# A channel attention kernel (384 x 384 x 384): the order of the second pass planned anew, and other row pitches in DRAM

## The chip, the cores and the metric

The kernel runs on one core of a Trainium2 chip. The metric is the device time of one execution in microseconds (us); lower is better. The kernel before takes 719.73 us, the median of three runs (719.13 to 720.23).

## The reference

```python
def reference(x, w1d):                       # x: (1, 384, 384, 384) bf16, w1d: (1,) bf16
    g = jnp.einsum("bhwc->bc", x) / (H * W)  # mean of each channel over all pixels
    s = _sigmoid(g * w1d[0])                 # k = 1: one tap
    return x * s[:, None, None, :]
```

(The padding and the loop over the taps are left out, since there is one tap.) The scale of each channel is known only when all of x has been summed. So x is read once for the sums, and every value has to be multiplied and written afterwards. x has 147,456 pixels of 384 channels, 113 MB in bf16, far more than the core's SBUF holds.

## The kernel before

**Rows.** A "row" is here one pixel (384 channels, 768 bytes) in each of the 128 partitions, 98,304 bytes together. A partition has 1,152 rows (`RPP`). The SBUF tile `arena` holds 275 of them (`ROWS`). DRAM is split in two chunks: `STREAMED`, the first 128 x 784 pixels, in which a partition's 784 rows lie behind one another, and `KEPT`, the other 128 x 368 pixels, with 368 rows a partition. So neighbouring partitions lie 784 or 368 rows apart in DRAM.

**First pass.** SP issues all loads on one queue. TensorE sums the rows as they land (`sum_rows`, one matmul with a matrix of ones for each row, accumulated in `bank0`). The streamed rows are loaded, summed and overwritten. The 368 kept rows stay on the core. Of these 72 (`N_RAW`) stay as they are, and 296 are packed in ten groups of 4q rows, q being 8 for eight "pair" groups (1 to 8), 6 for the group `BANKED` (9) and 4 for the group `FIRST` (0): VectorE folds each fourth row of a group into spare exponent bits of the three others (`fold`), in pieces of 4 rows (`PIECE`), so that 3q rows hold 4q. ScalarE tests that the exponents allow it and leaves the results in `seen`. The group `BANKED` is moved to PSUM. The odd groups lie in one column of the arena from row 12 up to `U` (108), the even ones in another from `G0` (116) up to `V` (212); each group's unfolded fourth quarter goes to the q rows just above its three quarters, which are the first rows of the group above it in the column, or the rows `U` to `U`+8 or `V` to `V`+8 at the top. The rows `A` (220), `T` (259) and `Y` (267) and up to 275 follow; `T` and `Y` are scratch.

**The turn.** ScalarE makes the scale `s_bf` from the sums (L445 to 449) and copies it to PSUM as `s_ps`.

**Second pass.** Everything in it is one multiplication by `s_bf` (`scale`, L461, on VectorE; three pieces of 4 rows at the start on GpSimd), then a store. The 72 raw rows come first. `unfold` takes a group's pieces apart again: with p = 4 a piece is five bit operations of 4 rows, one of 12, three joins of 4, and the multiplications of 12 and of 4. The 784 streamed rows are loaded again, scaled and stored, in the arena's free rows. These are few at first (47, as 204 hold folded groups, 16 wait for fourth quarters and 8 are scratch) and more with every group that has left.

**The planner.** The order of the second pass is worked out while the program is built: a loop steps a model clock by `DT` = 0.05 us and decides what VectorE does next and which load or store SP issues next, by model costs: `ROW` for a row moved, `PER_LOAD` and `PER_STORE` for a transfer, `SEEN` until a finished transfer is noticed, `TS` and `TT` for VectorE. What comes out is a fixed order of instructions on each engine, with semaphore waits; on the chip SP issues its transfers in that order, each as soon as what it needs is done. The class `Flow` records the steps and derives the waits.

In the planner before, VectorE scales landed rows while the backlog of transfers is below `PENDING` = 24 us, and otherwise starts a group. A store goes out as soon as its rows are scaled. A load is issued when a run of at least 32 idle rows is there (up to 48), or 8 rows with less than 9 us of backlog, or any with less than 4 us. The groups are taken alternately from the two columns: 7, 8, 5, 6, BANKED, 3, 4, 1, 2, FIRST. The first two are stored in two parts (12 and 20 rows), the others whole.

**The fallback.** `again` (L549) is a branch on GpSimd that redoes the kept rows where a test of `fold` failed. Its first instruction reads the flag. `Flow.emit` attaches one of a step's waits to the instruction that the step returns; `again` returns none (L568), so that one wait is left out.

Of the kernel before, what the change touches and what calls it, by code (L numbers as in the profile page):

```python
# [11 lines left out]
class Step:  # L12
    __slots__ = ("eng", "emit", "dma", "lane", "deps", "wanted", "rank", "waits", "know", "i")

    def __init__(self, eng, emit, dma):
        self.eng, self.emit, self.dma = eng, emit, dma
        self.deps, self.wanted, self.rank, self.waits, self.know = [], False, 0, [], None
        self.lane = None


class Flow:
# [12 lines left out]
    def add(self, eng, emit, reads=(), writes=(), dma=False, after=()):  # L34
        s = Step(eng, emit, dma)
        s.i = len(self.steps)
# [31 lines left out]
    def emit(self):  # L68
# [36 lines left out]
        last = {}  # L105
        with self.tc.tile_critical():  # L106
            for s in self.steps:
# [20 lines left out]
def kernel(  # L128
# [85 lines left out]
    STREAMED, KEPT = (0, N_STREAM), (N_STREAM, N_KEPT)  # L214
# [260 lines left out]
    def unfold(k, first):  # L475
# [10 lines left out]
        def fields():  # L486
            bits(u, w0, SHR, 4, AND, 0x0780, wc[0], uc)
            bits(b, w1, SHR, 8, AND, 0x0078, wc[1], bc)
            join(u, u, b, OR, uc + bc, uc)

        def signs():
            bits(c, w2, SHR, 12, AND, 0x0007, wc[2], cc)
            bits(b, w2, SHL, 4, AND, 0x8000, wc[2], bc)
            join(u, u, c, OR, uc + cc, uc)

        def three():
            wall = wc[0] + wc[1] + wc[2]
            bits(w, w, AND, 0x87FF, OR, 0x3800, wall, wall)
            join(u, u, b, OR, uc + bc, uc)
            scale(a, 3 * p)  # L500

        def fourth():

            bits(u, u, XOR, FIX, AND, 0xFFFF, uc, uc)
            scale(at, p + more)

        return [
            (fields, 2 * TS(p) + TT(p)),
            (signs, 2 * TS(p) + TT(p)),
            (three, TS(3 * p) + TT(p) + TT(3 * p)),  # L510
            (fourth, TS(p) + TT(p + more)),
# [68 lines left out]
    now = dve_at = 0.0  # L580
    moves, waiting, over, acts = deque(), deque(), deque(), deque()
    landed = deque()
    idle = [False] * ROWS
    todo = 0
    last_is_load = False

    def release(a, n):
        for i in range(a, a + n):
            idle[i] = True

    def runs():
        got, i = [], 0
        while i < ROWS:
            if idle[i]:
                j = i
                while j < ROWS and idle[j]:
                    j += 1
                got.append((j - i, i))
                i = j
            else:  # L600
                i += 1
        return got

    def send(chunk, a, lo, hi, then, known=None):

        waiting.append((dve_at, hi - lo, then, chunk, a, lo, [] if known is None else known))

    def backlog():
        return sum(e[1] for e in moves) + ROW * sum(e[1] for e in waiting)

    def split(n, m):
        k = -(-n // m)
        cuts = [n * i // k for i in range(k + 1)]
        return list(zip(cuts, cuts[1:]))


    SCRATCH = rows(Y, 8)
    needed = [set(SCRATCH + rows(U, 8)), set(SCRATCH + rows(V, 8)), set(SCRATCH)]

    def stored(a, n):  # L620

        def f():
            for i in range(a, a + n):
                for left in needed:
                    left.discard(("a", i))
                if not Y <= i < Y + 8 and not U <= i < U + 8 and not V <= i < V + 8:
                    idle[i] = True
        return f


    for a, n in (
        *((Y + i, 2) for i in range(0, 8, 2)), *((T + i, 2) for i in range(0, 8, 2)), (A + 26, 6), (A + 32, 7), (A + 13, 13), (V + 4, 4), (A, 13)
    ):
        landed.append((KEPT, a, raw(a), n, True))


    alongside = deque()
    t = 1.0
    for a, n in ((U, 4), (U + 4, 4), (V, 4)):
        scale(a, n, "POOL", after=[copied])  # L640
        t += 0.2 + 0.84 * n
        alongside.append((t, KEPT, a, raw(a), n))
# [5 lines left out]
    home = {g: i for i, column in enumerate(COLUMNS) for g in column}  # L648
    home[BANKED] = 2
    free = [True, True, True]  # L650
    total = len(GROUPS)
    out_rows = 0
    turns = deque()
    bank_at = None
    since = None
# [3 lines left out]
    def start_group():  # L659

# [3 lines left out]
        column = home[g]  # L664
        if needed[column] or not free[column] or g == BANKED and (bank_at is None or now < bank_at[1]):
            return False
        line.popleft()
        free[column] = False
        a, q = GROUPS[g]
        if g == BANKED:  # L670
            a = bank_at[0]

        below = 0
        if column < 2 and g != COLUMNS[column][0]:
            below = GROUPS[COLUMNS[column][COLUMNS[column].index(g) - 1]][1]

        def part():
            release(a + below, sent - below)

        def done():  # L680
            nonlocal out_rows
            out_rows += 1
            free[column] = True
            release(a + max(below, sent), n_rows - max(below, sent))

        for k in of_group(g):
            turns.extend(step + (None,) for step in unfold(k, a))
        sent, n_rows = 0, 4 * q + (g == BANKED)
        if len(line) >= total - N_SPLIT and q == PAIR:

            f, t, _ = turns[-6]
            sent = 3 * PIECE
            turns[-6] = (f, t, lambda: send(KEPT, a, c_group[g], c_group[g] + sent, part, written))
        f, t, _ = turns[-1]
        turns[-1] = (f, t, lambda: send(KEPT, a + sent, c_group[g] + sent, c_group[g] + n_rows, done, written))
        return True

    while True:

        if dve_at <= now:  # L700
            ahead = backlog()
            can = bool(turns)
            if not can and not alongside and (ahead >= PENDING or not landed):
                can = start_group()
            if landed and (ahead < PENDING or not can):
                chunk, a, lo, n, end = landed.popleft()
                scale(a, n, s=s_ps if alongside and now else s_bf)
                dve_at = now + TT(n)
                since = (a, lo) if since is None else since
                if end or ahead < MERGE:  # L710
                    b, first = since
# [99 lines left out]
```

## Time and profile before

| | us |
|---|---|
| median of the three runs | 719.73 |
| the profiled execution, its own time | 719.59 |
| its span, first to last instruction | 717.8 |
| VectorE busy in the span | 495.0 |
| TensorE busy | 212.8 |
| ScalarE busy | 116.5 |
| GpSimd busy | 9.4 |

The first pass ends at about 268 us with the activation that makes the scale (start 267.76 us). The page's slices are the span in 40 equal parts of 17.9 us. "SPq" is SP's queue of transfer instructions: a row of it gives the start of a stretch of issues, its length and their count. "[3.86 <-DMA ...]" behind a row is the idle time of that engine before it and what ended it. "DMA share" is the mean busy share of the core's 16 transfer engines; it can exceed 1 by some per cent in short windows. The 16 engines work each through its own part (8 partitions) of every transfer, in the order of the issues.

### The profile page before, as it was taken

What the parts mean: (1) busy time and instruction counts of PE and PEld (TensorE: products, weight loads), DVE (VectorE), ACT (ScalarE), POOL (GpSimd) and SP (SyncE); (2) the same over time, 40 slices, a digit from 0 to 9 for tenths busy, and PEclk for the clock granted to TensorE, in tenths of its full rate; (3) what the DMA queues carried; (4) which work ended last, traced back from release to release, by engine and by line L of the source; (5) the groups of instructions that cost most, each with busy time, mean ns of one, the idle gap of its engine ahead of it and who ended that gap; (6) DMA issues with size and microseconds to landing.
All of it is one profiled execution on the core that took longest, in us unless ns stands there. A gap on an engine that the chain in (4) does not pass through costs nothing.

```text
span 717.8 us, 2069 instructions
## 1 busy us (share of the span) xinstructions
PE 212.8 (30%) x1202; PEld 0.3 (0%) x3; DVE 495.0 (69%) x475; ACT 116.5 (16%) x97; POOL 9.4 (1%) x7
## 2 busy tenths in 40 slices
PE   4667879988787880000000000000000000000000
PEld 0000000000000000000000000000000000000000
DVE  4600001988998839989999999899999796035910
ACT  3700001666777620001000000000000000000000
POOL 0000000000000004000000000000000000000000
PEclk9898989999998995555555555555555555555555
DMA  9999999999999989999999999999999999999997
GB/s 378 438 438 436 438 436 419 437 431 426 423 430 425 429 331 389 404 432 423 429 428 433 431 431 430 432 429 443 428 435 430 429 436 434 436 432 432 434 433 314
DMA packets 20029, 303.69 MB, mean 423 GB/s; under 512 B 2226, under 2 KB 3506, under 8 KB 6578
## 3 DMA queue, kind: packets, MB, share of 16 engines
q1 hardware_dynamic: 20016, 303.57, 99.1%
q8 instruction: 4, 0.07, 0.0%
q14 instruction: 7, 0.06, 0.0%
q10 hardware_dynamic: 2, 0.00, 0.0%
HBM read 190.32 MB, written 113.25 MB: 423 GB/s over the span
## 4 chain that ended last, share of the span: by engine, by line
DMA 61%; DVE 22%; PE 8%; ACT 2%; issue 1%; SPq 0%; another core or an unknown queue 0%; DVEq 0%
DMA arena<-in_x_dram 47%; DVE arena L461 16%; DMA out_dram<-arena 14%; PE bank L241 8%; DVE arena L275 4%; ACT arena L312 2%; DVE arena L281 2%; SPq L235 0%; SPq L471 0%; ACT s_bf L448 0%; DVEq L112 0%; SPq L806 0%; SPq L112 0%; SPq L106 0%
## 5 line engine op out<-in xcount | busy, mean ns | idle before, releaser
L461 DVE TENSOR_TENSOR arena<-arena,s_bf 128x1536 bf16<-128x1536 bf16 (+9 forms) x96 | 228.4, 2411 | 70.7 <-DMA arena<-in_x_dram 58.0
L275 DVE TENSOR_SCALAR arena<-arena 128x1536 uint16<-128x1536 uint16 (+2 forms) x247 | 145.4, 634 | 106.8 <-DMA arena<-in_x_dram 100.7
L241 PE MATMUL bank<-arena,ones 128*128 128x384 bf16 x1151 | 204.5, 341 | 46.0 <-DMA arena<-in_x_dram 45.8
L281 DVE TENSOR_TENSOR arena<-arena 128x1536 uint16<-128x1536 uint16 (+2 forms) x114 | 121.3, 1064 | 9.7 <-PE bank L241 6.7
L312 ACT ACTIVATE arena<-arena 128x3072 uint16<-128x3072 uint16 (+1 forms) x38 | 102.5, 2696 | 144.7 <-DVE arena L275 144.7
L538 PE MATMUL bank<-odd,ones 128*128 128x1 bf16 x1 | 0.2, 187 | 325.6 <-DVE odd L533 325.6
L387 ACT COPY arena<-bank 128x512 uint32<-128x512 uint32 (+2 forms) x8 | 4.2, 534 | 69.3 <-DMA out_dram<-arena 69.1
L461 POOL TENSOR_TENSOR arena<-arena,s_bf 128x1536 bf16<-128x1536 bf16 x3 | 9.2, 3103 | 268.3 <-ACT bank L452 268.3
L461 DVE TENSOR_TENSOR arena<-arena,bank 128x768 bf16<-128x768 bf16 (+4 forms) x12 | 12.3, 1098 | 0.0
L241 PE MATMUL bank<-s_bf,ones 128*128 128x384 bf16 x48 | 8.3, 326 | 0.0
L312 ACT ACTIVATION_READ_ACCUMULATOR arena<-arena 128x1 f32 x38 | 7.1, 186 | 0.0
L387 ACT COPY bank<-arena 128x512 uint32<-128x512 uint32 (+2 forms) x8 | 3.8, 528 | 0.0
L255 PE MATMUL bank<-arena,ones 128*128 128x384 bf16 x1 | 0.5, 479 | 7.0 <-DMA arena<-in_x_dram 7.0
L448 ACT ACTIVATE s_bf<-bank,w_sc 128x384 bf16<-128x384 f32 x1 | 0.6, 581 | 11.2 <-PE bank L241 11.2
L779 ACT ACT_TABLE_LOAD x1 | 1.3, 1283 | 0.7 <-PEq L795 0.7
L332 DVE MEMSET ones<- 128x128 bf16 x1 | 0.2, 165 | 1.0 <-SPq L106 1.0
L337 PE MATMUL bank<-w_bf,ones 1*128 1x1 bf16 x1 | 0.2, 182 | 2.2 <-DMA w_bf<-in_w1d_dram 2.2
L342 DVE TENSOR_SCALAR w_sc<-bank 128x1 f32<-128x1 f32 x1 | 0.2, 158 | 0.9 <-PE bank L337 0.9
L538 PEld LDWEIGHTS bank<-odd,ones 128*128 128x128 bf16 x1 | 0.1, 105 | 583.9 <-DVE odd L533 583.9
L542 DVE CAST odd_i<-bank 128x1 int32<-128x1 f32 x1 | 0.2, 157 | 0.3 <-PE bank L538 0.3
L452 ACT COPY bank<-s_bf 128x192 uint32<-128x192 uint32 x1 | 0.3, 322 | 0.0
L387 ACT COPY arena<-rest 128x64 uint32<-128x64 uint32 x1 | 0.2, 244 | 0.0
(10 smaller groups left out, 1.4 us busy)
## 6 DMA issues: line engine op xcount, KB each, us to landing
arena<-in_x_dram SPq DMA_DIRECT2D x6, 6144.0 KB, 34.0
arena<-in_x_dram SPq DMA_DIRECT2D x6, 4608.0 KB, 29.4
out_dram<-arena SPq DMA_DIRECT2D x7, 3072.0 KB, 30.4
arena<-in_x_dram SPq DMA_DIRECT2D x6, 3072.0 KB, 25.2
arena<-in_x_dram SPq DMA_DIRECT2D x7, 2304.0 KB, 20.8
out_dram<-arena SPq DMA_DIRECT2D x3, 4608.0 KB, 37.3
arena<-in_x_dram SPq DMA_DIRECT2D x3, 4512.0 KB, 36.0
out_dram<-arena SPq DMA_DIRECT2D x3, 4512.0 KB, 34.4
```

The costliest lines, as they stand in the source:

```text
L241: return pe.add_instruction(mybir.InstMatmult(name=nc.get_next_instruction_name(), ins=[pe.lower_ap(rhs), pe.lower_ap(ones[:])], outs=[pe. ...
L255: return nc.tensor.matmul(acc, lhsT=ones[:], rhs=arena[:, i, :], start=first, stop=last)
L275: lambda: nc.vector.tensor_scalar(out=dst, in0=src, scalar1=s0, scalar2=s1, op0=op0, op1=op1),
L281: "DVE", lambda: nc.vector.tensor_tensor(out=dst, in0=a, in1=b, op=op), reads=reads, writes=writes
L312: lambda: nc.scalar.activation(out=y, in_=y, func=ACTF.Copy, accum_out=seen[:, 2 * k + i : 2 * k + i + 1]),
L332: fl.add("DVE", lambda: nc.vector.memset(ones[:], 1.0), writes=["ones"])
L387: "ACT", lambda: nc.scalar.copy(dst.bitcast(u32), src.bitcast(u32)), reads=reads, writes=writes
L448: lambda: nc.scalar.activation(out=s_bf[:], in_=acc, func=ACTF.Sigmoid, scale=w_sc[:, 0:1]),
L452: "ACT", lambda: nc.scalar.copy(s_ps.bitcast(u32), s_bf[:].bitcast(u32)), reads=["s_bf"], writes=["bank0"]
L461: lambda: vec.tensor_tensor(out=v, in0=v, in1=s[:, None, :].to_broadcast([P, n, C]), op=Op.mult),
L538: lambda: nc.tensor.matmul(votes, lhsT=ones[:], rhs=odd[:], start=True, stop=True),
L779: nc.scalar.preload_act_table(ACTF.Sigmoid)
```

## The change

Three things change.

1. **Row pitch.** The streamed chunk gets 785 rows a partition and the kept chunk 367. The additional streamed row is loaded last in the first pass, into the arena's last row, stays there, and is the first to be scaled and stored. The list of the last raw loads is shifted by one row.
2. **The planner.** Transfers are picked one at a time, once less than `DEPTH` = 6 us are queued in the model. Scaled rows wait in `ready`, where neighbours are joined to stores of up to 64 rows. Loads and stores alternate where both are possible; each waits until it has `aim` rows (half of the room, 8 to 48), unless less than `URGENT` = 2.5 us are queued. VectorE's pieces are 3 rows while little is queued, and up to 16 otherwise. `unfold` hands out its eleven operations one by one in place of four bundles; they are the same operations. The groups' order is 8, 6, 7, 5, 4, 2, 3, 1, BANKED, FIRST. A group is begun when the rows for its fourth quarter are free. All pair groups are sent in two parts, 12 and 20 rows, which join if the first still waits.
3. **The fallback** gets all its waits as instructions of their own (`block`).

```diff
+    def add(self, eng, emit, reads=(), writes=(), dma=False, after=(), block=False):
...
+                if s.block and hold:
+                    eng.wait_ge(*hold)
+                    hold = None
...
-    STREAMED, KEPT = (0, N_STREAM), (N_STREAM, N_KEPT)
+    STREAMED, KEPT = (0, N_STREAM + 1), (N_STREAM + 1, N_KEPT - 1)
+    LAST_ROW = ROWS - 1
...
-    for a, n in [(U, 8)] + S1 + [(A + 20, 11), (A + 31, 8), (V, 8), (Y + 2, 6), (T + 6, 4), (T + 3, 3), (T + 1, 2), (T, 1)]:
+    for a, n in [(U, 8)] + S1 + [(A + 20, 11), (A + 31, 8), (V, 8), (Y + 1, 6), (T + 5, 4), (T + 2, 3), (T, 2)]:
         take_raw(a, n)
+    load(STREAMED, LAST_ROW, N_STREAM, N_STREAM + 1)
+    sum_rows(LAST_ROW, 1)
...
-    ROW, PER_LOAD, PER_STORE = 0.2267, 0.112, 0.061
-    LAT, SEEN, DT = 0.4, 1.5, 0.05
-    PENDING, MERGE = 24.0, 12.0
-    BIG, CAP, PART, LOW, LAST = 32, 48, 16, 9.0, 4.0
-    DEEP, SHORT = 6.5, 1.0
-    BANKS_AT = 2
-    N_SPLIT = 2
+    ROW, PER_DMA = 0.2259, 0.08
+    ISSUE, LAT, SEEN, DT = 0.45, 0.9, 1.7, 0.05
+    PENDING, DEPTH, URGENT = 22.0, 6.0, 2.5
+    CAP, MOST, PART, FINE, LEAST = 48, 64, 16, 3, 8
+    THIRD = 2.0
+    BANKED_FROM = 7
...
+    def finish(chunk, a, lo, n, groups=0):
+        if ready:
+            e = ready[-1]
+            if e[0] is chunk and e[1] + e[3] == a and e[2] + e[3] == lo and e[3] + n <= MOST:
+                e[3] += n
+                e[4] += groups
+                return
+        ready.append([chunk, a, lo, n, groups])
...
+    def move(n):
+        nonlocal dma_at, sp_at
+        sp_at = now + ISSUE
+        dma_at = max(dma_at, now + LAT) + n * ROW + PER_DMA
+        return dma_at + SEEN
+
+    landed.append([STREAMED, LAST_ROW, N_STREAM, 1])
     for a, n in (
-        *((Y + i, 2) for i in range(0, 8, 2)), *((T + i, 2) for i in range(0, 8, 2)), (A + 26, 6), (A + 32, 7), (A + 13, 13), (V + 4, 4), (A, 13)
+        *((Y + i, 2) for i in (5, 3, 1)), *((T + i, 2) for i in (7, 5, 3)), (T, 3), (A + 26, 6), (A + 32, 7), (A + 13, 13), (V + 4, 4), (A, 13)
     ):
...
-    order = [g for i in (3, 2) for g in (1 + 2 * i, 2 + 2 * i)] + [BANKED]
-    order += [g for i in (1, 0) for g in (1 + 2 * i, 2 + 2 * i)] + [FIRST]
+    order = [8, 6, 7, 5, 4, 2, 3, 1, BANKED, FIRST]
...
+            supply = max(0.0, dma_at - now) + ROW * sum(e[3] for e in ready)
             can = bool(turns)
+            if not can and not alongside and (supply >= PENDING or not landed):
                 can = start_group()
+            if landed and (supply < PENDING or not can):
+                e = landed[0]
+                n = min(e[3], PART if supply > URGENT else FINE)
...
+        if sp_at <= now and dma_at - now < DEPTH:
+            ahead = dma_at - now
+            n, a = run_of_idle() if todo < N_STREAM else (0, 0)
             n = min(n, CAP, N_STREAM - todo)
+            room = space + in_flight
+            aim = min(CAP, max(LEAST, int(room / THIRD)))
+            have = ready[0][3] if ready else 0
+            load_ok = n and (n >= aim or n == N_STREAM - todo) and (todo or not landed)
+            store_ok = have and (have >= aim or ready[0][4] or len(ready) > 1 or ahead < URGENT)
+            waiting = sum(e[3] for e in landed)
+            if load_ok and not (last_is_load and store_ok):
+                pick = "load"
+            elif store_ok:
+                pick = "store"
+            elif load_ok:
+                pick = "load"
+            elif ahead < URGENT and n >= LEAST and (todo or not landed):
+                pick = "load"
+            else:
+                pick = None
```

More of the change, by code (lines that the diff above doesn't have):

```diff
@@ L601, in runs @@
                 i += 1
[L602 to L628, printed above, removed]
+        return best
+    def move(n):
[4 more added lines that the diff above has]
+    landed.append([STREAMED, LAST_ROW, N_STREAM, 1])
     for a, n in (
-        *((Y + i, 2) for i in range(0, 8, 2)), *((T + i, 2) for i in range(0, 8, 2)), (A + 26, 6), (A + 32, 7), (A + 13, 13), (V + 4, 4), (A, 13)
+        *((Y + i, 2) for i in (5, 3, 1)), *((T + i, 2) for i in (7, 5, 3)), (T, 3), (A + 26, 6), (A + 32, 7), (A + 13, 13), (V + 4, 4), (A, 13)
     ):
-        landed.append((KEPT, a, raw(a), n, True))
-    alongside = deque()
+        landed.append([KEPT, a, raw(a), n])
     t = 1.0
+    alongside = 0
     for a, n in ((U, 4), (U + 4, 4), (V, 4)):
@@ L688, in start_group @@
[L688 to L695, printed above, removed]
+        else:
+            busy4 = busy4 - set(range(a + 3 * q, a + 4 * q))
+        ks = of_group(g)
@@ L752 @@
-        if got and todo < N_STREAM:
-            n, a = max(got)
-            n = min(n, CAP, N_STREAM - todo)
-            ahead = backlog()
-            queue = sum(e[1] for e in moves)
-            turn = last_is_load or not todo or queue >= DEEP or queue < SHORT
-            if turn and (todo or not landed and not waiting) and (n >= BIG or n == N_STREAM - todo or (ahead < LOW and n >= 8) or ahead < LAST):
+            fl.add("POOL", again, reads=["odd_i", "s_bf"], writes=rows(Y, N_OVER), after=written, block=True)
```

218 lines of the change are left out of this document (122 added, 96 removed).

## The prediction

> **What bounds the kernel now.** I read the page's head first, then tables of windows by stage, then the timelines of TensorE, of the transfer queue and of GpSimd around the turn between the two passes.
>
> ```profile
> span 717.8 us, 2069 instructions
> GB/s 378 438 438 436 438 436 419 437 431 426 423 430 425 429 331 389 404 432 423 429 428 433 431 431 430 432 429 443 428 435 430 429 436 434 436 432 432 434 433 314
> q1 hardware_dynamic: 20016, 303.57, 99.1%
> ...
> 0.00:5.00 5.00, 0.18 (x1) 0.10 (x1) 0.53 (x3) 1.28 (x1) 0.20 (x4) 1.00 0.67 227
> 5.00:20.00 15.00, 9.68 (x41) 0.10 (x1) 9.52 (x15) 7.29 (x6) 0.00 (x0) 1.00 1.04 449
> ...
> 265.00:270.00 5.00, 2.72 (x17) 0.00 (x0) 1.63 (x4) 0.90 (x2) 1.23 (x1) 1.00 0.19 71
> 286.00:289.00 3.00, 0.00 (x0) 0.00 (x0) 3.00 (x3) 0.00 (x0) 0.00 (x0) 0.50 1.06 360
> 296.00:301.00 5.00, 0.00 (x0) 0.00 (x0) 4.73 (x3) 0.00 (x0) 0.00 (x0) 0.50 1.00 362
> 269.00:270.00 1.00, 0.00 (x0) 0.00 (x0) 1.00 (x3) 0.00 (x0) 1.00 (x1) 1.00 0.18 68
> 712.00:718.00 6.00, 0.00 (x0) 0.00 (x0) 0.00 (x0) 0.00 (x0) 0.00 (x0) 0.50 0.22 94
> 712.00:713.00 1.00, 0.00 (x0) 0.00 (x0) 0.00 (x0) 0.00 (x0) 0.00 (x0) 0.50 0.78 329
> 715.00:716.00 1.00, 0.00 (x0) 0.00 (x0) 0.00 (x0) 0.00 (x0) 0.00 (x0) 0.50 0.09 37
> 270.00:290.00 20.00, 0.00 (x0) 0.00 (x0) 19.93 (x21) 0.00 (x0) 8.00 (x3) 0.53 1.03 404
> 290.00:350.00 60.00, 0.00 (x0) 0.00 (x0) 54.84 (x49) 4.41 (x9) 0.00 (x0) 0.50 1.01 422
> 350.00:700.00 350.00, 0.19 (x1) 0.10 (x1) 280.01 (x211) 0.00 (x0) 0.00 (x0) 0.50 1.01 432
> 268.00:592.00 324.00, 0.00 (x0) 0.00 (x0) 308.28 (x264) 5.07 (x11) 9.23 (x3) 0.50 1.00 426
> 592.00:718.00 126.00, 0.19 (x1) 0.10 (x1) 48.13 (x19) 0.00 (x0) 0.00 (x0) 0.50 0.97 416
> ```
>
> In a window's row the last two numbers are the transfer engines' share and GB/s, the third busy time is VectorE. The transfer engines are full from 5 to 265 us and from 270 to 712 us; VectorE is nearly full up to 592 us (308.28 of 324) and idle most of the time after it (48.13 of 126). So the bound is bytes through the 16 transfer engines, and VectorE has 78 us of room behind the last group. A row of all 128 partitions is 98,304 bytes; 303.57 MB are 3,088 of them (1,152 loaded, 784 loaded again, 1,152 stored). Every transfer leaves 128 packets and 16 closing ones, so 20,016 packets are 139 transfers.
>
> The price of a row and of a transfer comes from landings in the first pass, where TensorE sits idle until a load lands:
>
> ```profile
> 53.67 10.56 PE L241 MATMUL bank<-arena,ones 128*128 128x384 bf16 x64 [2.34 <-DMA arena<-in_x_dram]
> 69.40 12.41 PE L241 MATMUL bank<-arena,ones 128*128 128x384 bf16 x64 [5.17 <-DMA arena<-in_x_dram]
> ...
> 98.35 13.28 PE L241 MATMUL bank<-arena,ones 128*128 128x384 bf16 x64 [3.92 <-DMA arena<-in_x_dram]
> 112.83 15.76 PE L241 MATMUL bank<-arena,ones 128*128 128x384 bf16 x96 [1.21 <-DMA arena<-in_x_dram]
> ...
> 243.78 5.36 PE L241 MATMUL bank<-arena,ones 128*128 128x384 bf16 x32 [1.53 <-DMA arena<-in_x_dram]
> 250.88 4.55 PE L241 MATMUL bank<-arena,ones 128*128 128x384 bf16 x27 [1.74 <-DMA arena<-in_x_dram]
> 257.27 10.45 PE L241 MATMUL bank<-arena,ones 128*128 128x384 bf16 x63 [1.84 <-DMA arena<-in_x_dram]
> ```
>
> One load of 64 rows takes 112.83 - 98.35 = 14.48 us, which is 434.5 GB/s. From 243.78 to 257.27 us, 59 rows land in four loads (12 of a group, 19, 8 and 20) in 13.49 us. With r for a row and c for a transfer, 64r + c = 14.48 and 59r + 4c = 13.49: c is 0.046 us, and I use 0.05; r is 0.2255.
>
> The span adds up: 3,088 x 0.2255 + 139 x 0.05 = 703.3 us. To that come, each as the window's length less its bytes at 434.5 GB/s, the start (0 to 20 us) 1.9, the turn (265 to 270) 4.2 and the tail (712 to 718) 4.7. Two dips right after the turn cost, against 432, 0.5 (286 to 289) and 0.8 (296 to 301). One 64-row load landed late, 69.40 - 53.67 = 15.73 in place of 14.48, 1.25 more. Together 716.6 of 717.8. The profiled execution took 719.59 (1.8 around the span); the three runs have a median of 719.73, 0.14 above, and lie 0.15% apart, so I call 0.2%, 1.44 us, the least that can be told from no change.
>
> **The change, part by part.** First pass: the loads keep their sizes, down to the last ten (8, 20, 11, 8, 8, 6, 4, 3, 2, 1); the last single row now comes from the streamed chunk into the arena's last row. Nothing is added: 0. The wait that the GpSimd fallback gains is on stores that are over long before the last stream stores: 0 while that holds, and if the last group's store came last, its return, which lies inside the tail's 4.7.
>
> The new row pitch: 785 and 367 rows in place of 784 and 368, 768 bytes more or fewer. Whether the addresses slow the transfers can only be bounded. From above by nothing gained: 64-row loads run at 434.5 with the old pitch, and the smaller ones differ by c alone. From below by a gain of 1.25 (the late landing) and of the gap between 432 and 434.5 over 350 us, 2.0, together 3.3. A loss can't be excluded either: loads that start at an odd row (the 19 and 20 above) show no more than c, so I bound it at one more c for each of 139 transfers, 7. The rows lie nearest to nothing: I take 0, and keep the gain as a rival.
>
> The turn. Here are the queues around it:
>
> ```profile
> 268.37 0.56 DVE L461 TENSOR_TENSOR arena<-arena,s_bf 128x768 bf16<-128x768 bf16 x1 [11.90 <-ACT s_bf L448]
> 268.77 9.23 POOL L461 TENSOR_TENSOR arena<-arena,s_bf 128x1536 bf16<-128x1536 bf16 x3 [268.33 <-ACT bank L452]
> 268.85 12.26 DVE L461 TENSOR_TENSOR arena<-arena,bank 128x768 bf16<-128x768 bf16 x12
> 268.96 12.51 SPq L471 DMA_DIRECT2D out_dram<-arena  x16
> 281.02 1.02 DVE L275 TENSOR_SCALAR arena<-arena 128x1536 uint16<-128x1536 uint16 x2
> 281.70 6.72 SPq L235 DMA_DIRECT2D arena<-in_x_dram  x3
> ...
> L461 DVE TENSOR_TENSOR arena<-arena,bank 128x768 bf16<-128x768 bf16 x7 | 3.3, 548 | 0.0
> L275 DVE TENSOR_SCALAR arena<-arena 128x4608 uint16<-128x4608 uint16 x18 | 24.4, 1353 | 0.0
> L461 DVE TENSOR_TENSOR arena<-arena,s_bf 128x4608 bf16<-128x4608 bf16 x28 | 71.1, 2553 | 5.0 <-DMA arena<-in_x_dram 5.0
> ```
>
> Before, VectorE scales 2 rows (0.56) and SP issues the first store. After, it scales 1 row first, an estimated 0.36, so that the first bytes leave 0.2 sooner; but then pairs follow every 0.55 as now, and a pair moves in 2r + c = 0.50, so VectorE sets the pace either way and after 16 rows both stand at 4.4 us. The order runs down the arena, so these pairs don't join; the 16 stores stay 16. Net 0, within 0.2 each way.
>
> Group order. The first group unfolded was 7, whose destination rows U GpSimd finishes early; it began at 281.02. Now 8 is first and needs rows V, the last of them GpSimd's third piece (done at 268.77 + 9.23 = 278.0), and they leave as the 15th store, 58 rows after the first bytes at about 269.8 (a share of 0.18 from 269 to 270): 58r + 15c = 13.8, so at 283.6, and the group starts once that is seen to be done, about 285, 4 us later than now. What is late next is its first 12 stored rows and then group 6, which waits for them. The cover is VectorE's room at the end; the same instructions take 1.35 and 2.55 where they took it before, only handed out one by one. So 0, and 4 us if that room were gone.
>
> Number of transfers. The second pass has now:
>
> ```profile
> L235 SPq DMA_DIRECT2D arena<-in_x_dram x32: 327/340/1197, 281.7 to 621.5; - x32
> DMA to landing us min/median/max: 10.7/17.8/54.0
> ...
> L471 SPq DMA_DIRECT2D out_dram<-arena x62: 332/343/1157, 269.0 to 684.6; - x62
> DMA to landing us min/median/max: 1.9/15.0/44.9
> ```
>
> Of 62 stores 16 are the raw rows', 12 the groups' (two of them in two parts), 34 the stream's. By the new rules: loads wait for half the free room, up to 48 rows; with 47 free rows at first and some 24 more with each group I count 11 small and 15 large, 26 in place of 32. Stream stores join up to 64 rows, about one for a load, 26 in place of 34. All groups are now sent as 12 and 20 rows unless the second part meets the first still waiting: about 15 in place of 12. Together 83 in place of 94. At c this is -0.55; it lies between 70 transfers (-1.2) and 96 (+0.1).
>
> The Trainium skill, "DMA: Bandwidth & Descriptors", section "Anatomy of one DMA", gives a transfer a fixed cost of about 2.0 us plus its bytes. By that, 11 fewer would save 22 us; the landings above show 0.05, so with a queue behind it nearly all of that cost is hidden, and the rule would matter only where the queue runs dry.
>
> The narrow stage. From 270 to 350 us the arena has 47 rows for the stream, and the rates are 404 and 422 where 432 comes later: 1.3 + 1.4 = 2.7 us, of which the two dips are 1.3 and the small stores most of the rest. The first loads are already here 21, 13 and 13 rows:
>
> ```profile
> arena<-in_x_dram SPq DMA_DIRECT2D x2, 1248.0 KB, 12.8
> arena<-in_x_dram SPq DMA_DIRECT2D x1, 2016.0 KB, 11.3
> ```
>
> The new plan sends the 21 rows ahead of the last raw store in place of all loads behind all stores, scales in smaller pieces while little is queued, and alternates. It can lose none of the 2.7 or about 2.0 (the stores of 2 rows stay); or it can open holes, the slower rival. I take the two dips, -1.3.
>
> Sum: 0 + 0 + 0 - 0.55 - 1.3 = -1.85; 719.59 - 1.85 = 717.74, say **717.8**. Its own range, by these bounds: 716.4 to 719.7.
>
> **The rivals.** *The shallow queue runs dry* (slower). The old plan issues 15 to 18 us (the medians above) ahead of landing, the new one only while less than 6 us are queued, and small pieces only below 2.5. The tail's rows show that the 16 engines don't end together: the share is 0.78 from 712 to 713 and still 0.09 from 715 to 716, a spread of some 3 us. Where a load waits for a store to return whole, the slowest engine decides, and the others stand still once 2.5 us are used up. From the first store (issued at 268.96 behind a scale that ended at 268.93) to the first bytes at 269.8 lie 0.9, which leaves 1.6 of margin, against that spread of 3: about 0.7 on average over the engines. A round over 47 rows (2 x 47 r, 21 us) has about three such issues, and there are some three rounds before group 8's rows come free, later than now by 4 us: 9 x 0.7 = 6; less what is saved with transfers, and in part where the dips are now, +3.5: 723. It decides once more than some three such waits exceed the margin. For it: the stage is a chain of store, load and scale already. Against: in the old trace the same 47 rows go round with a share of 1.01.
>
> *Nothing to win*: the transfer engines are full in both, the dips move elsewhere, groups in two parts eat the joined stores: 719.4. For it: shares of 1.00 and 1.01 nearly throughout. Against: the 1.3 of the dips has a place.
>
> *The pitch counts*: with the forecast's 1.85 also the 3.3 above: 714.5. Against it: 434.5 at the old pitch. The Trainium skill, same page, section "Latency and other measured facts", knows slow row pitches, at large powers of two, mended by 4 KiB more and not by 192 bytes. The old pitch, 602,112 bytes, is none of them, so that rule speaks against a gain; no run here shows such a pitch.
>
> **How the numbers follow.** Forecast 0.43, nothing to win 0.18, pitch 0.12, dry queue 0.27. Of the forecast about 0.7 lies below 718.3 (0.2% under the median), with the pitch 0.42 faster; the rest of the forecast and most of the second, 0.29, within; the dry queue and a little of the second, 0.29, slower. The range 715.0 to 723.0 leaves out half of the pitch's case and nearly half of the dry queue's, 0.18.
>
> **What would show it.** Right: some 83 transfers in the second pass (128 transfers, about 18,430 packets); windows after the turn at 415 GB/s and more with none near 360; 432 to 433 from 350 to 700; turn and tail as now; the groups over near 590. Wrong: shares below 0.95 between 290 and 350 (dry queue); 64-row landings under 14.4 us or 434 and more in mixed traffic (pitch), or over 15 (a pitch that hurts); groups that end after 680 would make VectorE the bound.

## The result and the profile after

The changed kernel takes 722.55 us (median of 22 runs, 720.07 to 724.27) where the one before takes 720.12 (719.13 to 722.18, 22 runs): a ratio of 1.0027, 95% interval 1.0019 to 1.0034. It is slower by 2.4 us; the forecast was faster by 1.9. The profiled execution took 721.51.

The head of the page after, and the windows by stage (the last two numbers are the transfer engines' share and GB/s, the third busy time is VectorE):

```profile
span 719.5 us, 2042 instructions
q1 hardware_dynamic: 17280, 303.57, 99.1%
...
265.00:270.00 5.00, 3.02 (x18) 0.00 (x0) 1.33 (x4) 0.90 (x2) 0.93 (x1) 1.00 0.35 132
286.00:289.00 3.00, 0.00 (x0) 0.00 (x0) 1.76 (x1) 0.00 (x0) 0.00 (x0) 0.50 1.03 432
296.00:301.00 5.00, 0.00 (x0) 0.00 (x0) 2.95 (x4) 0.00 (x0) 0.00 (x0) 0.50 0.99 365
270.00:290.00 20.00, 0.00 (x0) 0.00 (x0) 13.24 (x12) 0.00 (x0) 8.27 (x3) 0.53 1.01 384
290.00:350.00 60.00, 0.00 (x0) 0.00 (x0) 53.22 (x45) 0.00 (x0) 0.00 (x0) 0.50 1.01 410
350.00:700.00 350.00, 0.19 (x1) 0.10 (x1) 288.07 (x220) 4.41 (x9) 0.00 (x0) 0.50 1.00 433
334.00:341.00 7.00, 0.00 (x0) 0.00 (x0) 6.83 (x7) 0.00 (x0) 0.00 (x0) 0.50 0.98 359
```

17,280 packets are 120 transfers, 19 fewer. The same bytes went through the narrow stage more slowly: 384 from 270 to 290 us where it was 404, and 410 from 290 to 350 where it was 422, at a share of 1.01. From 334 to 341 us a new dip stands, 359 GB/s at 0.98; the kernel before has 424 there:

```profile
334.00:341.00 7.00, 0.00 (x0) 0.00 (x0) 6.97 (x10) 3.05 (x6) 0.00 (x0) 0.50 1.00 424
```

So the loss doesn't show as engines without packets, as a low share would, but as packets that take longer (their times stand in the last section).

The source view of the second pass's loads (first two lines) and stores, and SP's timeline and waits around the new dip:

```profile
L240 SPq DMA_DIRECT2D arena<-in_x_dram x23: 333/340/1767, 278.5 to 661.2; - x23
DMA to landing us min/median/max: 7.8/21.5/32.6
L478 SPq DMA_DIRECT2D out_dram<-arena x52: 332/343/1136, 269.1 to 695.2; - x52
DMA to landing us min/median/max: 1.6/13.8/40.1
```

```profile
317.73 0.34 SPq L240 DMA_DIRECT2D arena<-in_x_dram  x1
318.12 7.60 SPq L478 DMA_DIRECT2D out_dram<-arena  x2
332.01 0.34 SPq L240 DMA_DIRECT2D arena<-in_x_dram  x1
334.45 0.33 SPq L478 DMA_DIRECT2D out_dram<-arena  x1
...
SPq L240 <- DMA out_dram<-arena: 8.0, 2, 6.2
```

23 loads and 52 stores, 75 in place of 94. The load at 332.01 waited 6.2 us for a store to return whole; behind that store one of 20 rows was queued, 20 x 0.2255 + 0.05 = 4.56 us, and right after it comes the dip.

To place the loss I made a ledger from the trace's landings: for each transfer the mean over its 16 engines' landings, less that of the transfer before, less 0.2255 a row and 0.05 for itself. What is left is called lost. Each ledger is of one profiled execution. In us, for three profiles of each plan (of the new one the first run, its repeat and the one with the old pitch; of the old one the kernel before, the one with the new pitch, and the control with longer waits; all described below):

```
                    276-310 us   310-420 us   420 us on   transfers
new plan            2.55-2.78    2.42-4.11    0.37-0.44   120
old plan            1.65-1.81    0.16-0.34    0.53-0.64   137-139
```

New less old by their means: +1.0 at the turn, +2.9 from 310 to 420 us, -0.2 behind it, and -0.95 for 19 transfers at 0.05. The ledger has two more items, +0.6 in the first pass and -0.6 at the first store, but these come of taking means over the engines and all but cancel: the turn waits for the slowest engine, and the last load lands on that one at 267.36 us in the new plan and at 267.25 in the old (means of three). The last landing of all comes 2.9 later on average; its engines end 0.5 closer together, so the kernel ends 2.4 later.

### The profile page after: what moved, and what is told of

It is laid out like the page before. It is cut to its first block, busy times and chain, and to the rows that moved or that the text cites. A ratio compares the mean times of both kernels' runs of the same rounds, so it can differ in the third digit from the quotient of the medians.

```text
span 719.5 us, 2042 instructions
## 1 busy us (share of the span) xinstructions
PE 211.9 (29%) x1202; PEld 0.3 (0%) x3; DVE 494.3 (69%) x471; ACT 116.5 (16%) x97; POOL 9.4 (1%) x7
## 3 DMA queue, kind: packets, MB, share of 16 engines
q1 hardware_dynamic: 17280, 303.57, 99.1%
## 4 chain that ended last, share of the span: by engine, by line
DMA 67%; DVE 18%; PE 7%; ACT 2%; SPq 1%; issue 0%; another core or an unknown queue 0%; DVEq 0%
DMA arena<-in_x_dram 45%; DMA out_dram<-arena 23%; DVE arena L468 12%; PE bank L246 7%; DVE arena L280 4%; ACT arena L317 2%; DVE arena L286 2%; SPq L240 0%; SPq L478 0%; ACT s_bf L455 0%; SPq L113 0%; DVEq L113 0%; SPq L834 0%; SPq L107 0%
## 5 line engine op out<-in xcount | busy, mean ns | idle before, releaser
L468 DVE TENSOR_TENSOR arena<-arena,s_bf 128x6144 bf16<-128x6144 bf16 (+8 forms) x92 | 227.5, 2505 | 80.4 <-DMA arena<-in_x_dram 66.7
L468 DVE TENSOR_TENSOR arena<-arena,bank 128x768 bf16<-128x768 bf16 (+5 forms) x12 | 12.5, 1112 | 0.0
```

The source lines that it names most:

```text
L468: lambda: vec.tensor_tensor(out=v, in0=v, in1=s[:, None, :].to_broadcast([P, n, C]), op=Op.mult),
```

## The experiments

**Which part costs: the pitch or the plan?** Three kernels: the changed one again; the old planner with the pitches 785 and 367; the new planner, same list of transfers, with 784 and 368. The second in short:

```diff
-    STREAMED, KEPT = (0, N_STREAM), (N_STREAM, N_KEPT)
+    STREAMED, KEPT = (0, N_STREAM + 1), (N_STREAM + 1, N_KEPT - 1)
```

> The changed kernel once more, as the measure for the two below on the same chip: ratio to before 1.0027 within 0.001, about 2 us. In its record, packets that take over 1.1 times the usual time of their size should again stand mostly between 270 and 410 us and cost some 4 us over all 16 engines (before: 1.5), if they belong to the kernel; if they fall anywhere, they belong to the execution.

> The old planner with the new pitches of 785 and 367 rows alone. Theory A (the new order of transfers in the narrow stage after the turn costs the time; the pitch does nothing): ratio 1.000 within 0.0008. Theory B (the pitch slows single transfers, in loads and stores alike; the order does nothing): ratio 1.002 to 1.003, and slow packets that cost some 2 to 3 us more than before, some of them in the last loads of the first pass (250 to 260 us).

> The new planner with the old pitches of 784 and 368 rows; its transfers have the sizes and the order of the changed kernel. Theory A: ratio 1.002 to 1.003, with 405 to 415 GB/s from 290 to 350 us. Theory B: ratio 0.999 or less, since 19 transfers are saved (19 x 0.05 us = 0.95 us), with 420 GB/s or more from 290 to 350 us.

Measured: 1.0034 (1.0022 to 1.0046), 0.9998 (0.9988 to 1.0007), 1.0035 (1.0022 to 1.0049). The windows, first of the old planner with the new pitch, then of the new planner with the old one:

```profile
270.00:290.00 20.00, 0.00 (x0) 0.00 (x0) 19.93 (x20) 0.00 (x0) 7.74 (x3) 0.56 1.04 405
290.00:350.00 60.00, 0.00 (x0) 0.00 (x0) 55.20 (x49) 4.40 (x9) 0.00 (x0) 0.50 1.01 423
```

```profile
270.00:290.00 20.00, 0.00 (x0) 0.00 (x0) 12.87 (x11) 0.00 (x0) 7.90 (x3) 0.52 1.02 386
290.00:350.00 60.00, 0.00 (x0) 0.00 (x0) 53.17 (x45) 0.00 (x0) 0.00 (x0) 0.50 1.01 409
```

The repeat loses in the same places, more of it (4.1 us from 310 to 420 us where the first run lost 2.4). The rates go with the planner and not with the pitch. The pitch is worth nothing that can be measured; the plan costs all of it.

**What a change of direction and a short queue cost by themselves.** A kernel of transfers alone, in place of the whole computation: stages of mostly 16 transfers of 13 rows, each issued when the one k places before it has landed.

> Transfers alone, none of the computation: it loads parts of x and stores constant rows, so its output is not the reference's. Stages of 10 to 18 transfers, mostly of 13 rows (2.98 us each by 0.2255 a row and 0.05 a transfer), each transfer held back until the one k places before it has landed: load and store in turn with k = 2, 3, 4, 8; loads only and stores only with k = 3; two loads and two stores in turn with k = 4 and 8; 26 rows in turn with k = 3; in turn with k = 3 beside a busy VectorE; ten stores of 4 rows; and the turn's mixture of stores and first loads with k = 6. Theory 'lead' (a transfer that is issued with less than some 5 us queued ahead makes packets slow, though the queue never runs dry): 0.2 to 0.5 us lost for each transfer with k = 3 in every direction, nothing with k = 4 and 8. Theory 'direction' (each change between loads and stores costs time): 0.1 us or more a transfer at k = 8 in turn, half of it for pairs, nothing for loads only or stores only at k = 3. Theory 'place' (it is neither, but something of this kernel's second pass): 0.05 us or less everywhere but at k = 2.

Loads and stores in turn at k = 3, some 6 us queued ahead: after the first transfer, which starts on an empty queue, 0.25 us lost over 15, in pairs of +0.2 and -0.2. At k = 2, 3.0 to 3.5 us ahead: 3.9 us over 13, with single ones of 0.8 and 1.5. Loads only and stores only at k = 3 lost nothing. In turn at k = 4 and 8, with 26 rows, and beside a busy VectorE the losses came in such pairs too, 0.2 to 0.6 us in all over 9 to 15 transfers. 'Lead' and 'direction' both missed: k = 3 costs nothing, and neither do changes of direction once the two kinds alternate. The sums come nearest to 'place', which had a cost at k = 2 alone.

Two things there bear on the turn. The first change of direction after several transfers of one kind cost time with a long queue too: in the turn's mixture the last store before the first load lost 0.7 and that load 1.1, with 12 and 15 us queued; in the two stages of two loads and two stores the second load lost 0.8 and 1.0, with 5.0 us queued. And ten stores of 4 rows, issued with 1.9 to 3.2 us ahead, lost nothing.

**Rules of the plan, one at a time.** The first load held until the raw rows are sent; the old order of the groups; and all stores sent at once with DEPTH at 24 (three edits in one listing, in this order; the first changes the rule for short loads in the same way):

```diff
-            load_ok = n and (n >= aim or n == N_STREAM - todo) and (todo or not landed)
+            load_ok = n and (n >= aim or n == N_STREAM - todo) and (todo or not landed and not ready and not alongside)
...
-    order = [8, 6, 7, 5, 4, 2, 3, 1, BANKED, FIRST]
+    order = [7, 8, 5, 6, 3, 4, 1, 2, BANKED, FIRST]
...
-    PENDING, DEPTH, URGENT = 22.0, 6.0, 2.5
+    PENDING, DEPTH, URGENT = 22.0, 24.0, 2.5
...
-            store_ok = have and (have >= aim or ready[0][4] or len(ready) > 1 or ahead < URGENT)
+            store_ok = have
```

> The changed kernel, with the first load again held back until all raw rows have been scaled and sent. It shows whether the mixing of first loads and last raw stores is what costs. Theory 'mixing at the turn': of the changed kernel's 2.3 us over the old one, 0.6 to 1 us go, and the rate from 270 to 290 us is back at 400 GB/s or more; from 290 to 350 us it stays at 400 to 412. Theory 'lead': the same loss again at the other places, ratio to before 1.002 to 1.0035.

> The changed kernel with groups of both columns in turn (7, 8, 5, 6, 3, 4, 1, 2, the banked one, the first). Theory 'group order' (the 4 us that group 8 waits for its rows, and its slower release of rows, starve the narrow stage): ratio to before 1.001 or less and 418 GB/s or more from 290 to 350 us. Theory 'lead' (the late choice itself costs, whatever the order): ratio 1.002 to 1.0035, 400 to 412 GB/s there.

> The changed kernel with stores sent as soon as their rows are scaled and up to 24 us queued, so nothing is chosen late or joined; loads and group order stay. It has 154 transfers in place of 120, which alone costs 34 x 0.05 = 1.7 us. Theory 'lead': the losses at the turn and in the narrow stage (5.7 us after the turn in the changed kernel's record, 2.5 before) fall to 3 us or less, so that the ratio comes out at 1.001 to 1.002 in spite of the 1.7. Theory 'order' (the sequence of rows, not when they are issued): the losses stay at 5 us or more, ratio 1.004 to 1.006.

Measured: 1.0034 (1.0021 to 1.0046), 1.0041 (1.002 to 1.0063), 1.006 (1.0043 to 1.0076). Neither the mix at the turn nor the order of the groups alone gives the time back. But the rates did not stay where 'lead' had put them, at 400 to 412 GB/s from 290 to 350 us: all three have 421 or 422 there (as 'group order' had said of the second), and the loss from 310 to 420 us falls to 0.7, 0.5 and 0.3. Each rule also changes which transfers go out late, so these runs don't part the order from the lead. From 270 to 290 us the first has 384 GB/s, not the 400 of 'mixing'. Some of the loss is now elsewhere: each of these plans has one load of 48 rows issued with 4.54 to 4.55 us ahead, near 475 us, where the first plan has none, and each loses 0.7 to 1.8 us there. The third missed its expectation, and its ratio is the one that the rival 'order' gave: its losses after the turn fell to 4.1 us from 5.7 to 7.5, not to 3, and it makes 154 transfers (34 x 0.05 = 1.7 us more). That ledger is of the fastest of its four executions (722.74; the spans are 719.7, 720.3, 722.7 and 723.1), and this one took 3.0 us beyond its span where the changed kernel takes 2.0. So what the other three lost, and that microsecond, I can't place.

**The lead alone, in the kernel before.** Six transfers of the old plan are held until the one two places before them has landed; the control holds the same six for the one three places before.

```diff
+LATE = (73, 83, 98, 103, 113, 128)
...
+            if eng == "SP" and len(q) in LATE:
+                deps.add(q[-2])
```

> The kernel before, with its own plan; only six transfers of the second pass (its numbers 73, 83, 98, 103, 113 and 128 on the queue: three loads, three stores) are issued later, when the transfer two places before them has landed, so that one transfer of 16 or 20 rows is queued ahead of them: 3.7 to 4.6 us instead of 7 to 25 us. Theory 'short lead' (with the 16 engines 2.3 to 3.3 us apart, a transfer issued with less than about 4.6 us ahead of it loses 0.4 to 1.9 us): each of the six loses 0.3 to 1.9 us, 2.5 to 8 us in all, ratio 1.003 to 1.011. Rival 'order or place' (the slow spells of the new plan come from its order of loads and stores, or from the rows they touch, and the short lead only stands beside them): no loss above 0.3 us at the six places, ratio 0.999 to 1.001.

> The control: the same kernel and the same six transfers, each now held until the transfer three places before it has landed, so that two transfers (7.5 to 14.6 us) are queued ahead. Theory 'short lead': nothing is lost, ratio 0.999 to 1.001. If the added wait itself costs, whatever the lead, this loses as much as the kernel with one transfer ahead.

Measured: 1.010 (1.0084 to 1.0115), 7.4 us slower, and for the control 1.0002 (0.9993 to 1.0011). SP's timeline and two windows, first with the short lead, then of the control (128 is the load at 625.92, and at 609.86; the shorter window of each holds all of its move):

```profile
588.79 10.14 SPq L476 DMA_DIRECT2D out_dram<-arena  x2
625.92 0.34 SPq L240 DMA_DIRECT2D arena<-in_x_dram  x1
626.30 0.60 SPq L476 DMA_DIRECT2D out_dram<-arena  x1
...
628.00:642.00 14.00, 0.00 (x0) 0.00 (x0) 3.29 (x2) 0.00 (x0) 0.00 (x0) 0.50 1.03 402
350.00:700.00 350.00, 0.19 (x1) 0.11 (x1) 280.40 (x211) 0.00 (x0) 0.00 (x0) 0.50 1.00 423
```

```profile
593.46 0.33 SPq L476 DMA_DIRECT2D out_dram<-arena  x1
609.86 0.34 SPq L240 DMA_DIRECT2D arena<-in_x_dram  x1
610.25 0.66 SPq L476 DMA_DIRECT2D out_dram<-arena  x1
...
622.00:634.00 12.00, 0.00 (x0) 0.00 (x0) 2.38 (x1) 0.00 (x0) 0.00 (x0) 0.50 1.03 441
350.00:700.00 350.00, 0.19 (x1) 0.10 (x1) 280.30 (x211) 0.00 (x0) 0.00 (x0) 0.50 1.01 432
```

Around that load 402 GB/s stand against 441, at the same share of 1.03. Same rows, sizes and order in both, and an added wait in both: the lead is what costs. By the ledger the four with 3.6 us ahead lost, with the transfers right behind them, 1.6, 0.5, 1.2 and 2.2 us; two of them (103 and 113) had an echo of 1.0 in the second load that followed. Together 7.6, the whole difference. The two with 4.6 us, of 12 and 13 rows, lost nothing, which the expectation had not said.

How much is lost goes with the lead of the engine that is furthest ahead. In the table are the us queued ahead at the issue, for the slowest and the fastest of the 16; then what the transfer lost, and what it lost with the two behind it; number on the queue, L load or S store, rows. "Changed again" is the repeat; the runs of the rules are named by their rule:

```
                                slowest  fastest  lost  with two behind
changed        68 S13              4.99     2.49  0.02   0.01
changed        73 L26              4.60     2.42  0.18   0.31
short lead     83 S12              4.56     2.35  0.00   0.00
changed again  73 L26              4.58     2.29  0.85   0.89
sent at once  108 L48              4.54     2.22  0.74   0.76
old order      70 L13              4.73     2.21  0.07   0.10
old order     100 L48              4.54     2.18  0.86   0.95
changed        76 L21              4.55     2.04  1.17   1.24
changed        84 S26              4.59     1.91  0.12   0.55
short lead     98 L16              3.61     1.46  0.28   1.63
short lead    103 S16              3.58     1.24  0.01   0.65
changed again  76 L21              4.54     1.19  1.92   1.99
short lead    128 L32              3.61     1.12  1.97   2.00
load held      98 L48              4.55     1.03  1.78   1.82
short lead    113 S32              3.60     0.10  1.21   2.24
```

Behind 300 us, the profiles of whole kernels have 31 transfers issued with 5.1 us or less ahead for the slowest engine. The 16 of them with 2.3 us or more for the fastest lost at most 0.4, and 0.5 with the two behind; of the 15 below, 14 lost 0.5 to 2.2 with the two behind, and one small load 0.1. What the slowest has doesn't part them. This is a reading of where the losses stand: no run varied the fastest engine's lead alone, and at the turn it fails (behind the first two, the raw stores of 2 to 7 rows go out with 1.2 to 2.0 us ahead for every engine and lose nothing).

The first pass has a like case that no edit made. Load 36 on the queue (20 rows, with loads before and behind) went out with 5.4 or 5.5 us ahead for the slowest engine in five of the 13 profiles of whole kernels, four of the old plan and one of the new, and the three loads from it on lost 0.0 to 0.2 us; in the other eight, one of the old plan and seven of the new, it went out later, with 3.8 to 4.0 ahead, and they lost 0.4 to 1.1.

**The lead put back into the changed plan.** The bound on what is queued and the two rules for short transfers are raised: first all to 9.0, then to 8.0 (DEPTH), 4.0 (stores) and 5.0 (loads). The first:

```diff
-    PENDING, DEPTH, URGENT = 22.0, 6.0, 2.5
+    PENDING, DEPTH, URGENT = 22.0, 9.0, 2.5
...
-            store_ok = have and (have >= aim or ready[0][4] or len(ready) > 1 or ahead < URGENT)
+            store_ok = have and (have >= aim or ready[0][4] or len(ready) > 1 or ahead < 9.0)
...
-            elif ahead < URGENT and n >= LEAST and (todo or not landed):
+            elif ahead < 9.0 and n >= LEAST and (todo or not landed):
```

> The changed kernel with the bound DEPTH at 9.0 instead of 6.0 us, and with 9.0 in place of URGENT in the two rules that let a short store or load go (the rule for VectorE's small pieces keeps 2.5): loads and stores are issued with 8 to 9 us planned ahead from the narrow stage on, at the cost of 22 more transfers (97 picked in the second pass instead of 75). Theory 'short lead': the losses after 300 us fall from 3 to 5 us to under 0.6 us, the turn keeps its 2 to 2.8 us, and 22 x 0.05 = 1.1 us come back as transfers: 1.5 to 3.5 us faster than the changed kernel, ratio to the kernel before 0.999 to 1.001. Rival 'order or place': still alternating loads and stores in a new order, it keeps 5 to 7.5 us of losses after the turn and pays the transfers too: ratio 1.004 to 1.006.

> A milder form: DEPTH 8.0, a short store goes below 4.0 us and a short load below 5.0 us planned ahead, 86 transfers picked in the second pass, least planned lead 3.1 us (about 5.2 us on the chip, where 2.5 us planned became 4.6). Theory 'short lead': starts with 5 us and more ahead lose nothing, so losses after 300 us under 0.8 us, the turn 2 to 2.8 us, 0.55 us for the transfers: ratio 0.998 to 1.001. Rival 'order or place': 1.003 to 1.005.

Measured: 1.0007 (0.9998 to 1.0016) and 1.0009 (1.0 to 1.0018). Packets and windows of the first, then of the second:

```profile
q1 hardware_dynamic: 20448, 303.57, 99.2%
...
270.00:290.00 20.00, 0.00 (x0) 0.00 (x0) 13.21 (x12) 0.00 (x0) 8.25 (x3) 0.55 1.01 384
290.00:350.00 60.00, 0.00 (x0) 0.00 (x0) 54.64 (x48) 0.00 (x0) 0.00 (x0) 0.50 1.01 418
```

```profile
q1 hardware_dynamic: 18864, 303.57, 99.1%
...
270.00:290.00 20.00, 0.00 (x0) 0.00 (x0) 12.80 (x11) 0.00 (x0) 7.83 (x3) 0.54 1.02 384
290.00:350.00 60.00, 0.00 (x0) 0.00 (x0) 53.97 (x48) 0.00 (x0) 0.00 (x0) 0.50 1.01 419
```

From 310 to 420 us the ledger now has 0.3 and 0.6 us lost in place of 2.4 to 4.1; at the turn it still has 2.7 and 3.0. 20,448 packets are 142 transfers, 18,864 are 131: with 47 free rows, lead is bought with more and smaller transfers, and what the change saved is spent again. Most of the 2.4 us is back; neither beats the kernel before. Both plans also differ from the changed one in the sizes and the order of transfers; that the lead is what helped rests on the pair of runs above.

**The turn, in the kernel before.** The five transfers after the raw store of 13 rows are issued in another order (load 21, store 4, load 13, store 4, store 13 in place of the three stores and then the loads):

```diff
+        turn = [s for s in self.steps if s.dma and s.eng == "SP"][58:63]
+        at = sorted(self.steps.index(s) for s in turn)
+        order = [turn[i] for i in (3, 0, 4, 1, 2)]
+        for i, s in zip(at, order):
+            self.steps[i] = s
```

> The kernel before with five transfers at the turn in another order on the queue, nothing else: after the raw store of 13 rows it now issues the first load (21 rows), the store of 4, the load of 13, the store of 4, the store of 13, where it issued the three stores first and then the two loads. This is the way the changed plan mixes its first loads with the last raw stores. Theory 'changes of direction while the 16 engines are in step' (0.2 us apart there; the changed plan loses 2.5 to 3.1 us from 276 to 310 us, the one before 1.7): the loss in that stretch rises by 0.7 to 1.5 us to 2.4 to 3.2 us, ratio 1.001 to 1.002. Rival 'the turn costs what it costs' (a first change of direction and a second spell ten microseconds on, whatever the order; what the changed plan loses more is its 8-row load or its short waits): 1.5 to 2.0 us in that stretch, ratio 0.999 to 1.001.

Measured: 1.0062 (1.0048 to 1.0076), 4.7 us slower, more than either theory said. SP's waits from 284 to 300 us, and its timeline:

```profile
SPq L241 <- DMA out_dram<-arena: 15.7, 2, 12.0
...
297.23 0.34 SPq L241 DMA_DIRECT2D arena<-in_x_dram  x1
297.61 3.24 SPq L477 DMA_DIRECT2D out_dram<-arena  x4
```

The next load needs rows that the last of the reordered stores frees. Where it was, two loads stood behind that store (the next load had 7.9 us ahead); now nothing does: it waits 12.0 us, goes out as the queue ends, and loses 3.7 us, in a place where the old order loses 0.8. The two transfers of the first change of direction lost 0.9 and 0.7 where the old order lost 0.8 in all. So the mix costs some 0.8 us here, and the rest is a queue run dry. As a test of the turn by itself the run is spoiled. In the new plan the same two transfers lost 1.0 and 0.4 to 0.5, and in the transfers alone 0.7 and 1.1 with 12 us and more ahead, so this first loss needs no short lead; why the old order loses less there, and what makes up the changed plan's 1.0 us beyond it, is not settled.

## Why the prediction was wrong

**The bound** was right: bytes through 16 engines, with VectorE's room behind. **r and c** held (but the late landing of 1.25 was one engine of 16; the other 15 were on time, and it is there with the new pitch too, so it was no sign of the pitch): 64 rows still land in 112.84 - 98.34 = 14.50 us (TensorE's timeline after):

```profile
98.34 13.36 PE L246 MATMUL bank<-arena,ones 128*128 128x384 bf16 x64 [3.92 <-DMA arena<-in_x_dram]
112.84 15.76 PE L246 MATMUL bank<-arena,ones 128*128 128x384 bf16 x96 [1.14 <-DMA arena<-in_x_dram]
```

**Pitch**, taken as 0: right, 0.9998; the rival that it counts is dead. **First pass**, 0: right within 0.1, by the last landing. **The turn's first store**, 0 within 0.2: right. Counted from the last landing of the first pass, the first store lands 0.20 us sooner in every kernel that scales one row first, and the second 0.08 later.

**Group order**, 0 with VectorE's cover: right in the time, wrong in the size of the delay. VectorE around the turn, and the end of the last group:

```profile
286.36 1.76 DVE L468 TENSOR_TENSOR arena<-arena,s_bf 128x3072 bf16<-128x3072 bf16 x1 [4.87 <-DMA arena<-in_x_dram]
290.32 2.76 DVE L468 TENSOR_TENSOR arena<-arena,s_bf 128x4992 bf16<-128x4992 bf16 x1 [2.20 <-DMA arena<-in_x_dram]
293.00 1.02 DVE L280 TENSOR_SCALAR arena<-arena 128x1536 uint16<-128x1536 uint16 x2
...
657.39 0.19 PE L532 MATMUL bank<-odd,ones 128*128 128x1 bf16 x1 [389.38 <-DVE odd L527]
```

The first group starts at 293.0, not 285, and the last is done at 657, not near 590. The cover of 78 us took all of that, and the old order in the new plan (1.0041) was no better.

**Number of transfers**, -0.55 for 11 fewer: the price held (at 0.05 most transfers of the ledger lose nothing), the count was 19, so -0.95.

**The narrow stage**, -1.3, is the step that failed. I took the two dips after the turn as something that the new plan would remove. The one from 296 to 301 stands as it was (365 GB/s, before 362); the other only moved, as the rate from 270 to 290 fell to 384. Measured as the prediction did, against 432, the stage loses 2.2 + 3.1 = 5.3 us where it lost 2.7. And the step counted no price for what the plan does to get fewer transfers: it issues them late. Shown by the pair of runs in the old plan: lead taken from six transfers costs 7.4 us, the same waits with lead kept cost nothing. In the changed plan the loss from 310 to 420 us, 2.9 more than before, stands mostly at such late issues, and with the lead put back it is gone. The 1.0 at the turn has no shown cause.

**The dry queue**, the rival at 723, had the sign and the kind of cause: a wait for a store's return with too little left ahead. That it had nearly the time was luck, as its details were off. I expected nine waits of 0.7 within 270 to 350 us; there are about three that cost, of 0.1 to 1.9, up to 375 us, and the rest stands at the turn. I put the margin at 1.6 us from the 0.9 between an issue and the first bytes; behind 300 us the losses begin below 2.3 for the fastest engine. And I said that shares below 0.95 would show it; the share stays at 0.98 to 1.03 while the rate falls to 359. Reading shares alone, one would have called this stage full. The Trainium skill, "DMA: Bandwidth & Descriptors", section "Anatomy of one DMA", gives a fixed cost of about 2.0 us to a transfer; it gives it for transfers that GpSimd issues, while SP issues these. The prediction set it aside as hidden by the queue. The 2.3 us behind 300 us lie near that figure, the small stores at the turn do not fit it, and no run here shows that this cost is the reason.

**Nothing to win** had it right that the dips move, and missed the cost.

## What to carry to other kernels

Where transfers set the end, look at how much is queued at each issue and count it for the engine that is furthest ahead: here, behind the turn, 5 us for the slowest and 2.3 for the fastest cost 0.4 at most, and 3.6 for the slowest cost 0.5 to 2.2 us a time, as much as 10 to 44 saved transfers bring. Fewer, larger and later transfers out of a small buffer are a trade of lead against count, so price both. And a busy share near 1 doesn't rule out a queue that is too short (0.98 at 359 GB/s here); read GB/s beside it.

## What was not expected of the hardware

After a short lead the engines don't stand idle in the records: the packets of the load that was issued late take longer, a tenth of them about twice as long (13 of the 128 of the changed kernel's 76: 1,227 to 1,508 ns for 16,128 bytes where 601 is usual; 13 of 128 of number 128 with the short lead: 1,619 to 2,594 ns for 24,576 bytes where 912 is usual). An issue on an empty queue shows its first packet after 1.0 us (the load issued at 297.23 in the last run: 298.20), less than half of 2.3 us; what the rest is, no run shows.

The loss can come late: after two of the short starts it was in the second load that followed. At the turn, too, both plans lose twice, at the first change from stores to loads and again some 10 us on: 0.8 and 0.6 to 0.8 in the old plan, 1.4 to 1.5 and 1.1 to 1.2 in the new, and both times the engines, 0.2 us apart before the first, are further apart afterwards. That the engines being in step is what costs was not tried. Two losses of 0.6 us in the run with the old group order, with 25 us queued ahead, stay unexplained.
